# Hashed attention and a maxout FFN on one core: who sets the ones of the weight tiles, and where hashes and FFN groups stand in the order of work

## The chip, the core and the metric

The kernel runs on one core of a Trainium2 chip. The metric is the device time of one execution in microseconds (us). Five engines work beside each other, each through its own queue in order: TensorE (PE in the profile, its weight loads PEld), VectorE (DVE), ScalarE (ACT), GpSimd (POOL) and SyncE (SP), which here only issues DMAs.

## What is computed

Attention in which a query sees only the keys of its own hash bucket (six sign bits of a projection), and a feed-forward layer with a maximum over three branches, on 3072 tokens (4 batches x 768, 8 heads of 64):

```python
q_bits = (np.einsum('bhsd,dk->bhsk', q, proj) > 0).astype(np.int64)   # 6 bits; k_bits in the same way
mask = q_bucket[:, :, :, None] == k_bucket[:, :, None, :]
scores = np.where(mask, scale * np.matmul(q, k.transpose(0, 1, 3, 2)), -1e9)
attn = np.exp(scores - np.max(scores, axis=-1, keepdims=True))
attn = attn / (np.sum(attn, axis=-1, keepdims=True) + 1e-09)
x = np.matmul(attn, v)                       # then (b, s, h*d) = 3072 x 512
h = np.maximum(np.maximum(x @ w1, x @ w2), x @ w3)    # 512 -> 768
out = h @ w_out                                       # 768 -> 512
```

## The kernel before, in words

**Bits instead of a mask.** Each head's keys and queries lie as columns of a tile `S`: 64 rows hold the scaled vector and some rows below it hold the hash bits as plus or minus one half. One matmul over all rows gives the score plus a term that is largest where all bits agree, and the exponential (L303, with a bias) drives all other pairs to nothing.

**Units.** A unit is a piece of scores: one head, one chunk of queries, some blocks of 128 keys. Batch 0 has three chunks of 256 queries and 16 units per chunk; the other batches have two chunks of 384 and 24 units per chunk. That makes 192 units, 48 a batch, and chunks 0 to 8. For each unit `scores` (L279) issues the matmuls (L295, three of 256 columns or two of 384) into one of two PSUM buffers, takes a weight tile from the list `at_free`, and ScalarE writes the exponentials into it (L303). There are 24 weight tiles `AT`, used in turn.

**Ones in the weight tiles.** Behind each block of 256 or 384 columns stand two columns of ones; where a chunk is the first of its batch and half, the values' matmuls read one of them too (`n = w + 1`, L368), which gives the sum of the values. The tiles start in the form of batch 0 (blocks of 256). When a tile is first taken for a block of 384, the ones lie elsewhere, and `scores` has VectorE set them (L300 to L302), just ahead of the exponential on ScalarE.

**Bursts.** When four heads of a chunk (a half, i = 0 or 1) are through, a burst follows (L338): sums of the weights by a matmul with ones (L350), VectorE's transposes and reciprocal (L357 to L361), and the weighted values in two sides (L372), normalised by VectorE into `xT` (L379). Sums and values use four 32-column tiles of TensorE beside each other. From chunk 3 on VectorE adds the weights of a head's units first (L326, and L329 from chunk 5 on), so that fewer sums are left to TensorE. At the end of the burst's second side the weight tiles are given back to `at_free` (L382 to L385). In batch 0 the bursts of the second half are placed at units 32, 40 and 48; from chunk 3 on one comes every 12 units: 63, 75, 87, 99, 111, 123, 135, 147, 159, 171, 183 and one after the last unit.

**FFN groups.** When a chunk is complete its FFN is cut into groups (L390): 18 of four matmuls (L401; a copy of the first branch, then two maxima on VectorE, L406 to L410) and, per 128 rows, two halves of three matmuls (L445), the second of which ends with a copy on ScalarE and a store. At each unit a credit of 1 (batch 0) or 1.15 groups is spent from the list `ffn`. What is left of it when the units are through, and the whole FFN of chunk 8, come behind the last burst (L604 to L609). Scores, hashes, bursts and FFN groups that need a PSUM bank beside the score buffers share four of them, taken and given back in turn.

**Hashes.** Heads of batch 0 are turned on TensorE and hashed in pairs or one by one (L166 to L184), with the copies split over engines. From group 2 on (a group is four heads; groups 2g and 2g+1 belong to batch g) GpSimd or SP loads the group (L187), VectorE transposes it in four steps a side (L200), GpSimd narrows it (L205), SP places it into `S` (L210), TensorE hashes it (L219), VectorE makes bits (L222), and SP sends them into `S` (L230), at least one unit later. Which unit each of these steps stands at is written by hand: for groups 4 to 7 the first transpose is at `SPREAD[batch][0]` and they are `SPREAD[batch][1]/4` units apart, loads start 14 units before, and the hash stands at `need - 9`, where `need` is the unit that first reads the group's scores (96, 108, 144, 156).

**The order.** The whole order is the order of the calls (`manual_schedule`). In the loop over units (L586) each turn issues the scores of the next unit, then the steps listed for this one (`at`), then FFN groups by credit, then bursts (`todo`), then a hash (`hash_at`). Ahead of the loop (L486 to L520) stands the start: the first head's two sides are turned, copied, placed and hashed in two halves each, and score 0 is issued.

Of the kernel before, what the change touches and what calls it, by code (L numbers as in the profile page):

```python
# [17 lines left out]
def kernel(  # L18
# [12 lines left out]
    nc = tc.nc  # L31
# [4 lines left out]
    HALF = S // 2  # L36
# [14 lines left out]
    SCALE = 0.125 / (RS * RS)  # L51
    EPS = 2.0 ** -60
    NAT = 24
    SPREAD = {2: (61, 9), 3: (100, 12)}
    THIRD_ADD = 5
    LAG = (1, 4)
    ATW = 776
# [23 lines left out]
    at_tiles = [konst.tile([P, ATW], FP16, name=f"AT{i}", tag=f"AT{i}") for i in range(NAT)]  # L81
# [8 lines left out]
    def bank():  # L90
        i = free_banks.pop(0)
        return i, bank_tiles[i]

    def give(i):
        free_banks.append(i)
# [23 lines left out]
    def pair_turn(pi, side, hd, mp):  # L119
        n = nat[pi].rearrange("p (s h w) -> p s h w", s=2, h=2)  # L120
        for i in range(MH):
            nc.tensor.transpose(mp[:, i * P : (i + 1) * P], n[:, side, hd, i * P : (i + 1) * P], iden[:])  # L122
# [132 lines left out]
    def parts_of(c):  # L255
        return chunks[c][2] * NM // (2 * HALF)
# [4 lines left out]
    NU = len(units)  # L261
# [5 lines left out]
    at_free = list(range(NAT))  # L267
    at_form = [THIRD] * NAT
    at_of = {}
    xts, sv_of = {}, {}  # L270

    def blocks(t, w):
        nb = 2 * HALF // w
        return t[:, 0 : nb * (w + 2)].rearrange("p (n c) -> p n c", n=nb)

    def block_of(b, m):
        return 2 * (m % MH) + m // MH if b == 0 else m

    def scores(u):  # L279
        c, h, part = units[u]  # L280
        b, q0, w = chunks[c]
        nb = 2 * HALF // w
        (qn, qx), (kn, kx) = where[0, b * H + h], where[1, b * H + h]
        bits = NBITS if b == 0 else KB
        sc = sc_ps.tile([P, 2, 512], FP32, tag="sc", name="sc")
        if w == HALF:
            views = [sc[:, j, 0:w] for j in range(nb)]
            whole = sc[:, :, 0:w]
        else:
            flat = sc.rearrange("p a c -> p (a c)")  # L290
            views = [flat[:, j * w : (j + 1) * w] for j in range(nb)]
            whole = flat[:, 0 : nb * w].rearrange("p (n c) -> p n c", n=nb)
        for j in range(nb):
            m = nb * part + j
            nc.tensor.matmul(views[j], s_of[kn][0 : D + bits, kx, m * P : (m + 1) * P],  # L295
                             s_of[qn][0 : D + bits, qx, q0 : q0 + w], start=True, stop=True)
        i = at_free.pop(0)
        at_of[u] = i
        t = blocks(at_tiles[i], w)
        if at_form[i] != w:  # L300
            nc.vector.memset(t[:, :, w : w + 2], 1.0)
            at_form[i] = w  # L302
        nc.scalar.activation(t[:, :, 0:w], whole, ActFn.Exp, bias=-SCALE * 0.25 * bits, scale=SCALE)  # L303

    unit_at = {e: u for u, e in enumerate(units)}

    def weights_of(c, h, m):
        w = chunks[c][2]
        nb = 2 * HALF // w
        return blocks(at_tiles[at_of[unit_at[c, h, m // nb]]], w)[:, m % nb, :]  # L310
# [20 lines left out]
    def sum_blocks(c, h):  # L331
        w = chunks[c][2]
        if (c, h) in sum_of:
            t = sum_of[c, h]
            return [t[:, j, 0:w] for j in range(1 if c >= THIRD_ADD else 2)]
        return [weights_of(c, h, m)[:, 0:w] for m in range(NM)]

    def burst(c, i):  # L338
        b, q0, w = chunks[c]
        held = {}  # L340
        rb = []

        def sums(m0, m1):
            if m0 == 0:
                held["s"] = bank()
            sm = held["s"][1]
            bs = [sum_blocks(c, 4 * i + x) for x in range(4)]
            for m in range(len(bs[0])):
                for x in range(4):
                    nc.tensor.matmul(sm[Q * x : Q * (x + 1), 0:w], ones[:, :], bs[x][m],  # L350
                                     start=(m == 0), stop=(m == len(bs[0]) - 1))
            if m1 == NM:
                ys = ys_pool.tile([P, HALF], FP32, tag="ys", name="ys")
                rr = small.tile([P, HALF // Q], FP32, tag="rr", name="rr")
                n = w // Q
                rb.append(rb_pool.tile([P, HALF], FP32, tag="rb", name="rb"))
                nc.vector.transpose(ys[:, 0:w], sm[:, 0:w])  # L357
                give(held["s"][0])
                nc.vector.tensor_scalar(out=rr[:, 0:n], in0=ys[:, 0:w:Q], scalar1=EPS * S, scalar2=None, op0=AluOp.add)
                nc.vector.reciprocal(rr[:, 0:n], rr[:, 0:n])  # L360
                nc.vector.transpose(rb[0][:, 0:w], rr[:, 0:n].unsqueeze(2).to_broadcast((P, n, Q)))  # L361

        def values(side, m0, m1):
            if m0 == 0:
                held[side] = bank()
            av = held[side][1]
            first = (b, i, side) not in sv_of
            n = w + 1 if first else w  # L368
            for m in range(m0, m1):
                cb = block_of(b, m)  # L370
                for x in range(4):
                    nc.tensor.matmul(av[Q * x : Q * (x + 1), 0:n], v_at[2 * b + i][:, x, cb * D + side : (cb + 1) * D : 2],  # L372
                                     weights_of(c, 4 * i + x, m)[:, 0:n], start=(m == 0), stop=(m == NM - 1))
            if m1 == NM:
                if first:
                    sv_of[b, i, side] = small.tile([P, 1], FP32, tag=f"sv{side}", name="sv")
                    nc.vector.tensor_scalar(out=sv_of[b, i, side][:], in0=av[:, w : w + 1], scalar1=EPS, scalar2=None,
                                            op0=AluOp.mult)
                nc.vector.scalar_tensor_tensor(out=xt_of(c)[:, 2 * i + side, 0:w], in0=av[:, 0:w],  # L379
                                               scalar=sv_of[b, i, side][:], in1=rb[0][:, 0:w], op0=AluOp.add, op1=AluOp.mult)  # L380
                give(held[side][0])
                if side == 1:  # L382
                    for h in range(4 * i, 4 * i + 4):
                        for n in range(parts_of(c)):
                            at_free.append(at_of[unit_at[c, h, n]])  # L385

        return sums, values

# [71 lines left out]
    with tc.manual_schedule():  # L460
# [27 lines left out]
        ib, bk = bank()  # L488
# [13 lines left out]
        head_hash(mk, 0, 1, 0, (1,))  # L502
        head_bits(mk, 0, 1, 0, 1)
        give(ik)
        scores(0)
        pair_turn(0, 1, 1, bk)
        head_hash(mq, 0, 0, 0, (1,))
        head_bits(mq, 0, 0, 0, 1)
        give(iq)
        pair_turn(0, 0, 1, bq)  # L510
        pair_keep(0, 1, 1, bk)
        give(ib)
# [34 lines left out]
        hash_at = {}  # L547
        for g in range(2, NQUAD):
            b2, i2 = divmod(g, 2)
            need = UPB * b2 + 12 * i2  # L550
            for n, side in enumerate((1, 0)):
                name = (side, g)
                if g > 3:
                    us = [SPREAD[b2][0] + SPREAD[b2][1] * (8 * i2 + 4 * n + n2) // 4 for n2 in range(4)]
                    for x in range(4):
                        when(us[0] - 14 + x, load_quad, side, g, (x,), nc.gpsimd)
                else:
                    us = [need - {2: 26, 3: 23}[g] + 4 * n + n2 for n2 in range(4)]
                for n2, u2 in enumerate(us):
                    when(u2, turn, name, n2 // 2, n2 % 2)  # L560
                    if n2 % 2:
                        when(u2 + 1, narrow, name, n2 // 2)
                when(us[3] + 3, place, name, range(4))
            hash_at[{2: 33, 3: 47}.get(g, need - 9)] = g
            when({2: 36, 3: 46}.get(g, need - 22), load_v, g)

        ffn, credit = [], 0
        todo = {}
        last_of = {}
        for c, i in sorted(done_at, key=lambda e: done_at[e]):  # L570
# [3 lines left out]
            for n, f in enumerate(pieces):  # L574
                u = {(0, 0): (20, 21, 22), (1, 0): (24, 25, 26), (2, 0): (28, 29, 30)}.get((c, i), (d, d, d))[n]
# [8 lines left out]
                when(min(u + 2, NU - 1), add, c, h, n)  # L584

        for u in range(NU):  # L586
            if u + 1 < NU:
                scores(u + 1)
            for f in at.pop(u, []):
                f()  # L590
            for c in ffn_at.get(u, []):
                ffn += ffn_groups(c)
            credit += 1 if u < UPB else 1.15
            if not ffn:
                credit = 0
            while ffn and credit >= 1:
                credit -= 1
                ffn.pop(0)()
            for f in todo.pop(u, []):
                f()  # L600
            if u in hash_at:
                when(u + 1, quad_hash(hash_at[u]))

        for u in sorted(todo):  # L604
            for f in todo[u]:
                f()
# [33 lines left out]
```

## Time and profile before

| | |
|---|---|
| time, three runs | 272.11, 272.56, 272.76 us (median 272.56) |
| profiled execution | 272.63 us |
| its span, first to last instruction | 270.9 us |
| busy | PE 96%, PEld 57%, DVE 77%, ACT 66%, POOL 25% |
| granted TensorE clock | 1.00 in all 40 slices |
| HBM read, written | 25.17 MB, 6.29 MB |
| hashes of groups 2 to 7 start on TensorE at | 43.0, 57.7, 106.4, 124.4, 171.9, 187.9 us |

All positions in time are us from the span's start. In the view of waits a line names the waiting engine and line, what ended the wait, and then the total, the number of times and the longest. In a timeline a line has start, duration, engine, line, operation, tiles and shapes, count, and in brackets the idle time before it and what ended that. The busy digits are tenths in 40 slices of 6.8 us each.

### The profile page before, as it was taken

How to read it: one execution, taken by the hardware profiler on the slowest of the kernel's cores; microseconds unless marked ns; L12 is line 12 of the kernel's file. 1: busy time of each engine (PE TensorE's matmuls, PEld its weight loads, DVE VectorE, ACT ScalarE, POOL GpSimd, SP SyncE). 2: the span in 40 equal slices, each digit the busy share in tenths (PEclk: the TensorE clock that was granted, in tenths of full speed). 3: DMA queues.
4: the chain of work that ended last, by engine and by line, in shares of the span. 5: the costliest groups of instructions: out<-in, count | busy, mean ns of one | idle time of the engine just before them, and what ended most of it. 6: DMA issues, size and time to landing. Idle time of an engine off the chain costs nothing.

```text
span 270.9 us, 6455 instructions
## 1 busy us (share of the span) xinstructions
PE 259.4 (96%) x2505; PEld 154.5 (57%) x2505; DVE 208.9 (77%) x517; ACT 177.6 (66%) x257; POOL 68.4 (25%) x108
## 2 busy tenths in 40 slices
PE   7899999999989999979999999999999999998995
PEld 3555567865756575545555555565555655554553
DVE  2777686967699899948999998799849795887351
ACT  3587776676939693963959768484895859580322
POOL 3489641272032435140141512011000000000000
PEclk9999999999999999999999999999999999999999
DMA  6969999959623863980036291801130003000303
GB/s 204 315 137 160 221 255 229 229 80 250 150 72 88 156 173 38 235 218 20 11 91 202 30 205 69 169 11 46 29 116 2 2 2 116 2 0 2 116 0 116
DMA packets 20717, 30.95 MB, mean 114 GB/s; under 512 B 2608, under 2 KB 15248, under 8 KB 20688
## 3 DMA queue, kind: packets, MB, share of 16 engines
q0 software_dynamic: 8128, 13.37, 26.3%
q1 hardware_dynamic: 12128, 16.66, 21.1%
q10 hardware_dynamic: 432, 0.52, 0.5%
q8 instruction: 19, 0.31, 0.5%
q14 instruction: 10, 0.08, 0.1%
HBM read 25.17 MB, written 6.29 MB: 116 GB/s over the span
## 4 chain that ended last, share of the span: by engine, by line
PE 86%; DVE 5%; ACT 3%; DMA 2%; POOL 2%; issue 1%; SPq 0%; DVEq 0%; ACTq 0%; POOLq 0%
PE ms L401 32%; PE sc L295 22%; PE ms L372 11%; PE ms L445 10%; PE ms L350 3%; PE ms L219 3%; ACT AT L303 3%; DMA S<-bits 2%; PE ms L483 1%; POOL S L136 1%; PE ms L149 1%; PE ms L122 1%; DVE ad L326 1%; PE ms L169 1%; DVE S L174 1%
## 5 line engine op out<-in xcount | busy, mean ns | idle before, releaser
L303 ACT ACTIVATE AT<-sc 128x768 f16<-128x768 f32 x192 | 152.7, 816 | 65.6 <-PE sc L295 57.9
L401 PE MATMUL ms<-xT,w_sb 128*128 128x384 f16 (+1 forms) x648 | 115.0, 307 | 0.0
L295 PE MATMUL sc<-S 72*128 72x384 bf16 (+1 forms) x432 | 93.5, 308 | 5.4 <-ACT AT L303 2.5
L401 PEld LDWEIGHTS <-w_sb 128*128 128x128 f16 x648 | 62.6, 97 | 35.8 <-issue 0.3
L410 DVE TENSOR_TENSOR ht<-ht,ms 128x384 f16<-128x384 f16 (+1 forms) x108 | 54.2, 504 | 26.0 <-PE ms L401 23.1
L295 PEld LDWEIGHTS <-S 72*128 72x128 bf16 (+1 forms) x432 | 39.4, 98 | 38.0 <-issue 14.1
L205 POOL TENSOR_SCALAR T<-T 128x768 bf16<-128x768 f32 x24 | 22.9, 953 | 105.2 <-DVE T L200 64.5
L372 PE MATMUL ms<-AT,vo 128*32 128x385 f16 (+3 forms) x864 | 35.5, 309 | 0.0
L445 PE MATMUL ms<-wout_sb,ht 128*128 128x512 f16 x138 | 35.3, 378 | 0.0
L372 PEld LDWEIGHTS <-vo 128*32 128x32 f16 x864 | 22.8, 96 | 10.5 <-issue 2.9
L326 DVE TENSOR_TENSOR ad<-ad,AT 128x768 f16<-128x768 f16 x48 | 26.6, 553 | 1.8 <-ACT AT L303 1.1
L200 DVE STREAM_TRANSPOSE T<-nat 128x384 f32<-128x384 f32 x48 | 26.9, 565 | 0.0
L326 DVE TENSOR_TENSOR ad<-AT,AT 128x768 f16<-128x768 f16 x48 | 26.2, 546 | 0.4 <-ACT AT L303 0.4
L406 ACT CAST ht<-ms 128x384 f16<-128x384 f32 x36 | 17.2, 477 | 8.8 <-PE ms L401 8.8
L379 DVE SCALAR_TENSOR_TENSOR xT<-ms,sv,rb 128x384 f16<-128x384 f32 (+1 forms) x36 | 19.8, 567 | 1.6 <-PE ms L372 0.2
L445 PEld LDWEIGHTS <-ht 128*128 128x128 f16 x138 | 13.3, 97 | 13.0 <-DVE ht L410 0.4
L449 ACT COPY osb<-ms 128x512 f32<-128x512 f32 x21 | 12.2, 582 | 8.3 <-PE ms L445 7.2
L329 DVE TENSOR_TENSOR ad<-ad 128x384 f16<-128x384 f16 x32 | 15.5, 484 | 1.1
L136 POOL TENSOR_SCALAR S<-T 64x384 bf16<-64x384 f32 (+1 forms) x23 | 14.2, 617 | 4.7 <-DVE T L131 3.1
L357 DVE STREAM_TRANSPOSE ys<-ms 128x384 f32<-128x384 f32 (+1 forms) x18 | 9.6, 535 | 6.5 <-PE ms L350 6.4
L174 DVE TENSOR_SCALAR S<-ms 6x384 bf16<-6x384 f32 x16 | 8.9, 554 | 3.8 <-PE ms L169 3.5
L194 POOL DMA_DIRECT2D nat<-in_q_dram x20 | 11.1, 564 | 2.1 <-DMA vo<-in_v_dram 2.0
(48 smaller groups left out, 122.8 us busy)
## 6 DMA issues: line engine op xcount, KB each, us to landing
out_dram<-osb SPq DMA_DIRECT2D x21, 256.0 KB
S<-T SPq DMA_DIRECT2D x48, 96.0 KB
nat<-in_q_dram POOLq DMA_DIRECT2D x20, 192.0 KB, 7.3
vo<-in_v_dram POOLq DMA_DIRECT2D x8, 384.0 KB, 6.4
nat<-in_k_dram POOLq DMA_DIRECT2D x16, 192.0 KB, 6.5
w_sb<-in_moe_w_dram POOLq DMA_DIRECT2D x3, 768.0 KB, 7.6
nat<-in_k_dram SPq DMA_DIRECT2D x10, 192.0 KB
nat<-in_k_dram SPq DMA_DIRECT2D x3, 384.0 KB
```

The costliest lines, as they stand in the source:

```text
L136: nc.gpsimd.tensor_scalar(out=o, in0=i_, scalar1=RS, scalar2=1.0, op0=AluOp.mult, op1=AluOp.mult)
L200: nc.vector.transpose(t32[name][:, u, half * HALF : (half + 1) * HALF], i_)
L205: nc.gpsimd.tensor_scalar(out=t16[name][:, u, :], in0=t32[name][:, u, :], scalar1=RS, scalar2=1.0, op0=AluOp.mult, op1=AluOp.mult)
L295: nc.tensor.matmul(views[j], s_of[kn][0 : D + bits, kx, m * P : (m + 1) * P], s_of[qn][0 : D + bits, qx, q0 : q0 + w], start=True, stop=True)
L303: nc.scalar.activation(t[:, :, 0:w], whole, ActFn.Exp, bias=-SCALE * 0.25 * bits, scale=SCALE)
L326: nc.vector.tensor_tensor(out=sum_of[c, h][:], in0=t[0], in1=t[n], op=AluOp.add)
L372: nc.tensor.matmul(av[Q * x : Q * (x + 1), 0:n], v_at[2 * b + i][:, x, cb * D + side : (cb + 1) * D : 2], weights_of(c, 4 * i + x, m)[:, 0 ...
L379: nc.vector.scalar_tensor_tensor(out=xt_of(c)[:, 2 * i + side, 0:w], in0=av[:, 0:w], scalar=sv_of[b, i, side][:], in1=rb[0][:, 0:w], op0=A ...
L401: nc.tensor.matmul(ps[:, 0:w], w_sb[wi][:, jc, fb * P : (fb + 1) * P], xt[:, jc, 0:w], start=(jc == 0), stop=(jc == NJC - 1))
L406: nc.scalar.copy(hts[fb][:, 0:w], ps[:, 0:w])
L410: nc.vector.tensor_tensor(out=hts[fb][:, 0:w], in0=hts[fb][:, 0:w], in1=ps[:, 0:w], op=AluOp.max)
L445: nc.tensor.matmul(ps[:, 0:DM], hts[fb][:, tb * P : (tb + 1) * P], wout_sb[:, fb, :], start=(fb == 0), stop=(fb == NFB - 1))
```

## The change

The diff has four parts. The ones are set by GpSimd when the second-half bursts of batch 0 give their tiles back, and the tile is marked as being in the form of 384 columns. The hashes of groups 4 to 7 stand at `need - 12`, which are units 84, 96, 132 and 144 instead of 87, 99, 135 and 147, and the transposes of batch 3, with their loads, narrowings and placements, start at unit 97 instead of 100. The first three FFN groups that are left after the last unit are issued ahead of the last burst. In the start, the hash of the first head's second query half stands ahead of score 0, and score 1 directly behind score 0, instead of in the first turn of the loop.

```diff
-    SPREAD = {2: (61, 9), 3: (100, 12)}
+    SPREAD = {2: (61, 9), 3: (97, 12)}
...
                         for n in range(parts_of(c)):
-                            at_free.append(at_of[unit_at[c, h, n]])
+                            a = at_of[unit_at[c, h, n]]
+                            if b == 0 and i == 1:
+                                nc.gpsimd.memset(blocks(at_tiles[a], HALF)[:, :, HALF : HALF + 2], 1.0)
+                                at_form[a] = HALF
+                            at_free.append(a)
...
         head_bits(mk, 0, 1, 0, 1)
         give(ik)
-        scores(0)
-        pair_turn(0, 1, 1, bk)
         head_hash(mq, 0, 0, 0, (1,))
         head_bits(mq, 0, 0, 0, 1)
         give(iq)
+        scores(0)
+        scores(1)
+        pair_turn(0, 1, 1, bk)
         pair_turn(0, 0, 1, bq)
...
-            hash_at[{2: 33, 3: 47}.get(g, need - 9)] = g
+            hash_at[{2: 33, 3: 47}.get(g, need - 12)] = g
...
         for u in range(NU):
-            if u + 1 < NU:
+            if 0 < u < NU - 1:
                 scores(u + 1)
...
+        for f in ffn[:3]:
+            f()
+        ffn = ffn[3:]
         for u in sorted(todo):
             for f in todo[u]:
                 f()
```

## The prediction

> **What bounds the kernel now.** I read the busy times first, then the waits of TensorE, then the neighbourhood of each wait, because a busy share alone hides what a stage waits for.
>
> ```profile
> PE 259.4 (96%) x2505; PEld 154.5 (57%) x2505; DVE 208.9 (77%) x517; ACT 177.6 (66%) x257; POOL 68.4 (25%) x108
> ...
> PE   7899999999989999979999999999999999998995
> ...
> DVE  2777686967699899948999998799849795887351
> ```
>
> TensorE is busy nearly everywhere, so a microsecond is won only where it stands still or switches. The second candidate is VectorE, with nines from slice 10 to 17 (68 to 122 us). TensorE's own waits:
>
> ```profile
> PE sc L295 <- ACT AT L303: 2.5, 4, 1.2
> PE sc L295 <- DMA S<-bits: 1.7, 1, 1.7
> PE ms L350 <- DVE ad L329: 1.2, 1, 1.2
> ...
> PE ms L350 <- DVE ad L326: 0.4, 1, 0.4
> ```
>
> Drawn ends of matmuls are modelled, so I measure a loss by starts: in dense stretches the next matmul starts 0.109 us after one of 256 columns and 0.162 us after one of 384. What exceeds that is lost.
>
> **Part 1, ones by GpSimd (L301 goes; 24 memsets in the bursts of units 32, 40, 48).** ScalarE waits for VectorE's memset in the view of waits, and TensorE then waits for ScalarE to free a score buffer:
>
> ```profile
> ACT AT L303 <- DVE AT L301: 5.4, 4, 3.3
> ```
>
> (us in total, times, longest). The longest is this one, in the timeline:
>
> ```profile
> 80.64 1.62 ACT L303 ACTIVATE AT<-sc 128x768 f16<-128x768 f32 x2 [3.27 <-DVE AT L301]
> ```
>
> The memset ahead of it (80.45) takes 0.06 us, but it stands in VectorE's queue behind a burst's normalisation (77.43 to 80.42 here). By starts TensorE loses 80.00 to 81.50 less 0.11 = 1.39, in the same way 63.52 to 64.22 less 0.11 = 0.59, and 0.13 and 0.09 at 85 and 86: 2.20 us. On GpSimd each memset is 16 units ahead of its reader: tiles freed in the burst at 41 to 43 us are read by unit 48 (57.6), those at 60 to 62 by unit 64 (76.6). All 24 VectorE memsets disappear, since exactly these 24 tiles are the ones changing form. With the exponential of unit 65 starting at about 79.1 instead of 80.64, the next thing late is VectorE: the window 91 to 103 shows
>
> ```profile
> 91.00:103.00 12.00, 12.00 (x133) 8.56 (x132) 11.65 (x31) 9.13 (x12) 2.87 (x4) 1.00 0.69 154
> ```
>
> (busy PE, PEld, DVE, ACT, POOL: VectorE 11.65 of 12). It gains 0.59 itself before 68 us, about 0.03 for each memset taken from its saturated stretch (start to start of an add and the evacuation behind it: 0.47 with a memset between, 0.44 without), 0.4 in all, and an idle 0.95 at 89.6 to 90.6 where it waited for TensorE: 1.9 against TensorE's 2.2. I take **-2.2**, keep +0.2 for this friction, and as bounds -2.2 and -0.8 (VectorE takes the 1.39 back).
>
> GpSimd's price: its memsets take 0.10 to 0.20 us (rows L624, L518, 128x64 at 0.15). The added ones are bounded by these below and, above, by 0.55 us, a DMA issue on that engine. Behind them queue two loads of values, the narrowing of group 3 and the third and fourth quarter-loads of group 4's keys. The latter are the nearest due: issued at 59.1 and 59.65 now, they would follow the burst that ends at 62.1, so 62.1 + 8 x 0.15 + 2 x 0.56 = 64.4, landing 6.5 later (median of that group) at 70.9. The transpose that reads them starts at 73.84, or 73.25 after the gain: 2.3 us of cover, gone if one memset costs over 0.15 + 2.3/8 = 0.44.
>
> **Part 2, later hashes three units earlier.** Hash of group 4 (unit 87) comes behind a burst; its bits are issued by SP from 109.0 to 111.9 and TensorE stands until 117.15:
>
> ```profile
> 117.15 0.50 PE L295 MATMUL sc<-S 72*128 72x384 bf16 x2 [1.69 <-DMA S<-bits]
> ```
>
> By starts 115.13 to 117.15 less 0.16: **-1.85**. In unit 84 TensorE reaches the hash at 101.2 instead of 106.4; VectorE, 2 us behind there, gives bits at 103.6, SP's four issues (0.73 each) end by 106.6, ahead of the S placements now at 104.8, and with the 5.2 from last issue to landing now seen they are there by 112. Cover: 3 us. At 103.4 the burst waits 0.53 for an add; a hash of 1.5 us ahead of it gives VectorE that time, less 0.56 for the bits: **-0.5**, between -0.53 and +0.3. Groups 5, 6, 7 show no wait for bits now, so nothing is won there. Their new neighbour is the last transpose, two units before the hash (group 5: unit 94 and 96). Group 5's starts at 114.18 and ends at 114.75; TensorE would come to the hash at about 117.2: 2.4 us of cover. For group 7 the two-unit distance existed before (145, 147), and SPREAD's 97 keeps it (142, 144); its loads, narrowing and placements move by the same three units.
>
> But a hash is a job in 32-column tiles, like the burst. These rows price the switch (burst with hash, burst without, hash alone):
>
> ```profile
> 122.48 2.12 PE L372 MATMUL ms<-AT,vo 128*32 128x384 f16 x48
> 124.43 1.46 PE L219 MATMUL ms<-T,pj 128*32 128x384 f32 x16
> 125.83 0.50 PE L295 MATMUL sc<-S 72*128 72x384 bf16 x2
> ...
> 139.14 2.15 PE L372 MATMUL ms<-AT,vo 128*32 128x385 f16 x48
> 141.22 0.50 PE L295 MATMUL sc<-S 72*128 72x384 bf16 x2
> ...
> 42.56 0.50 PE L295 MATMUL sc<-S 70*128 70x256 bf16 x3
> 43.00 1.50 PE L219 MATMUL ms<-T,pj 128*32 128x384 f32 x16
> 44.43 0.50 PE L295 MATMUL sc<-S 70*128 70x256 bf16 x3
> ```
>
> Behind a burst: (125.83 - 122.48) - (141.22 - 139.14) = 3.35 - 2.08 = 1.27. Alone: 44.43 - (42.56 + 3 x 0.109) = 1.54. So each parted hash costs 0.27 more, four **+1.0** (bounds 0.8 and 1.1).
> The Trainium skill, "TensorEngine Tiling (Array Packing)", Key Properties, says that changing the tiling mode drains TensorE, which speaks against this part; it gives no price, and the rows agree in direction. By a reading without any drain the total would be 1.0 us lower.
>
> **Part 3, three FFN groups before the last burst.** TensorE starts a sum at 243.69 and the next at 245.19:
>
> ```profile
> 245.19 0.32 PE L350 MATMUL ms<-ad,ones 128*32 128x384 f16 x1 [1.16 <-DVE ad L329]
> ```
>
> The three groups are one of L401 (0.65) and two halves of L445 (0.65 each), 1.95 us, more than the gap of 1.5. They don't fill it whole: the sixth matmul of L445 reads the hidden tile whose last two maxima stand in VectorE's queue behind the adds, which end at 245.14; 0.5 each brings 246.1. TensorE would stand from 245.16 to about 246.15. Counting work, before: 245.19 + burst 2.2 + L401 0.65 + six halves 3.9 = 251.94; after: 246.35 + 2.3 + four halves 2.6 = 251.3. **-0.65**, between 0 and -1.35. The normalised tile now comes 1.07 us after the burst; the four halves (2.6) cover that.
>
> **Part 4, first hashes ahead of scores.** Score 0 waits anyway (7.94, behind placements and bits), so the moved hash is free. Score 1 goes from 9.81 to about 8.5 (its bits end at 8.39), the fourth bits from 9.61 to 8.4, the copies of the second heads from 10.19 to 9.25. Behind them TensorE is in order: two transposes, two groups, then score 2 at about 10.3 instead of 10.80; from exponential 2 (11.33) ScalarE runs without a long gap to 19.4. **-0.5**, between 0 and -1.1 (what the exponential of unit 1 wins).
>
> **Sum.** -2.2 + 0.2 - 1.85 - 0.5 + 1.0 - 0.65 - 0.5 = -4.5 us; from the profiled execution's 272.63 (span 270.9 and 1.7 around it), 268.1. The median of the runs is 272.56, 0.07 lower, so I say **268.0**.
>
> **Rivals.**
> VectorE takes it back: nines from 68 to 122 us speak for it, the idle 0.95 and the shifted hash against. It gives back 1.39 and 0.5: 269.9. Chance 0.17.
> Port: two VectorE adds (88.17 and 112.33) took 0.99 instead of 0.55 beside a narrowing on GpSimd. If each of the eight last memsets waits half a microsecond for VectorE, they take 8 x 0.7 = 5.6, the keys land at 75.3, 2 us late: 270.0. Chance 0.08.
> The Trainium skill, "SBUF — State Buffer", section "SBUF: two separate sides", says that GpSimd and VectorE share a port pair as an exclusive lock, and that a two-input VectorE operation conflicts only with a GpSimd one that reads; a memset reads nothing, so by it only the other VectorE modes could hold a memset up.
> More is won (tail fully covered, start 1.1): 266.7. Chance 0.10.
> Nothing moves, because the exponentials wait for GpSimd as they did for VectorE: then only the other parts count against +1.0; with the tail and start at zero 271.9 to 272.6. Chance 0.04.
> **Slower:** the same queue on GpSimd, with memsets so slow that group 4's transposes hold VectorE, and everything behind them. Place: after unit 48's burst. Price: 8 x (m - 0.44) us. It ends above the time before from m = 1.0, where 4.5 is lost; at 1.3 it is 274.9. Rows of 0.10 to 0.20 speak against it. Chance 0.08.
> The forecast has 0.53.
>
> The range is **266.2 to 270.8**: the larger gain, both 270 rivals, and the bounds of start, tail and friction. A measurement here tells 0.2% (0.5 us). Faster 0.88, within 0.2% 0.04, slower 0.08.
>
> **What would show it.** No L301 on VectorE; ScalarE without a wait for ones at 80 us; no wait for bits at 115; hashes standing between scores; the last sums without their wait, but one in L445 before them; exponential 1 at 9.2. I am wrong if TensorE's waits for VectorE between 75 and 115 us grow by over 1 us, or the transposes of group 4 wait for their load.

## The result, and the profile after

The changed kernel takes 269.21 us (median of 4 runs, 268.47 to 270.15), beside 272.66 us for the kernel before on the same chips. The ratio is 0.9869, with a 95% interval from 0.9824 to 0.9915. The profiled execution took 269.23 us, with a span of 267.2. The forecast of 268.0 had the direction and the range (266.2 to 270.8) right; it promised 4.5 us, and 3.4 came.

In the changed file lines 386 and later have moved: L387 is GpSimd's memset, L405 is the old L401, L414 the old L410, L449 the old L445. From the page of the changed kernel, the busy times:

```profile
PE 259.1 (97%) x2505; PEld 153.5 (57%) x2505; DVE 208.7 (78%) x493; ACT 177.9 (67%) x257; POOL 70.1 (26%) x132
```

VectorE has 24 instructions less and GpSimd 24 more, and nobody's busy time has changed by 2 us. TensorE's own waits, from the view of waits (us in total, times, longest):

```profile
PE ms L449 <- DVE ht L414: 1.6, 3, 0.8
...
PE sc L295 <- ACT AT L303: 0.8, 2, 0.6
PE sc L295 <- DVE S L174: 0.8, 2, 0.6
```

The waits for bits and for the adds are gone, that for exponentials has shrunk from 2.5 to 0.8, and there is a new one: the output matmuls (L449) wait for hidden tiles on VectorE.

**Where the time went** can be read without any cause in mind from when the first score matmul of a unit starts (TensorE's L295) in each profile. Every change of the difference is a gain or a loss between two units:

| unit | before | after | difference | what lies between it and the row above |
|---|---|---|---|---|
| 0 | 7.94 | 7.86 | -0.08 | |
| 3 | 11.21 | 10.51 | -0.70 | part 4 |
| 32 | 39.57 | 38.88 | -0.69 | |
| 34 | 42.56 | 42.09 | -0.47 | a loss of 0.22 inside the burst of unit 32 |
| 52 | 64.22 | 63.15 | -1.07 | part 1: the wait at 63.5 |
| 62 | 73.34 | 72.11 | -1.23 | part 1, small waits |
| 68 | 82.31 | 79.65 | -2.66 | part 1: the wait at 80 |
| 74 | 88.00 | 86.16 | -1.84 | new waits for VectorE |
| 84 | 99.47 | 97.63 | -1.84 | |
| 90 | 109.00 | 106.68 | -2.32 | part 2: group 4's hash parted from the burst, adds no longer late |
| 94 | 112.69 | 110.71 | -1.98 | a new wait for VectorE |
| 96 | 117.15 | 113.32 | -3.83 | part 2: the wait for bits |
| 102 | 126.81 | 123.21 | -3.60 | group 5's hash parted from its burst |
| 138 | 174.25 | 170.89 | -3.36 | the same, group 6 |
| 150 | 190.92 | 187.81 | -3.11 | the same, group 7 |
| 191 | 241.97 | 238.85 | -3.12 | |
| last matmul | 267.43 | 263.84 | -3.59 | part 3 |

The lines that answer to those of the prediction, from the changed kernel's timeline. ScalarE at the place where it waited 3.27 us for ones:

```profile
77.94 3.88 ACT L303 ACTIVATE AT<-sc 128x768 f16<-128x768 f32 x5 [2.47 <-PE sc L295]
```

It now waits for the scores alone and runs five exponentials one behind the other. TensorE around group 4's hash and the burst of unit 87:

```profile
99.25 1.50 PE L219 MATMUL ms<-T,pj 128*32 128x384 f32 x16
100.68 0.50 PE L295 MATMUL sc<-S 72*128 72x384 bf16 x2
...
103.08 0.51 PE L350 MATMUL ms<-ad,ones 128*32 128x384 f16 x8
103.42 2.12 PE L372 MATMUL ms<-AT,vo 128*32 128x384 f16 x48
105.47 0.34 PE L295 MATMUL sc<-S 72*128 72x384 bf16 x1
```

The hash stands between scores, the eight sums run in one piece, and the bits are there when unit 96 needs them (its scores start at 113.32 without a wait). Before, the sums of unit 87's burst stood still behind the third:

```profile
103.40 0.34 PE L350 MATMUL ms<-ad,ones 128*32 128x384 f16 x3
104.09 0.48 PE L350 MATMUL ms<-ad,ones 128*32 128x384 f16 x5 [0.35 <-DVE ad L326]
```

From the first sum to the first value it took 1.03 us before and takes 0.34 now, so this wait cost 0.69. The prediction has 0.53, which is less by the 0.16 that two matmuls of 384 columns are apart elsewhere; but four sums in tiles beside each other start within 0.01 us of one another. The end:

```profile
241.13 1.24 PE L449 MATMUL ms<-wout_sb,ht 128*128 128x512 f16 x5
243.20 0.39 PE L449 MATMUL ms<-wout_sb,ht 128*128 128x512 f16 x1 [0.82 <-DVE ht L414]
243.52 0.35 PE L350 MATMUL ms<-ad,ones 128*32 128x384 f16 x4
```

The sums no longer wait; the sixth output matmul ahead of them does. The start:

```profile
7.86 0.49 PE L295 MATMUL sc<-S 70*128 70x256 bf16 x3 [0.60 <-DVE S L174]
8.55 0.49 PE L295 MATMUL sc<-S 70*128 70x256 bf16 x3 [0.20 <-DVE S L174]
```

And the new loss, TensorE first and then VectorE:

```profile
84.76 0.59 PE L449 MATMUL ms<-wout_sb,ht 128*128 128x512 f16 x2
85.94 0.39 PE L449 MATMUL ms<-wout_sb,ht 128*128 128x512 f16 x1 [0.58 <-DVE ht L414]
```

```profile
84.54 0.57 DVE L200 STREAM_TRANSPOSE T<-nat 128x384 f32<-128x384 f32 x1
85.03 0.52 DVE L326 TENSOR_TENSOR ad<-ad,AT 128x768 f16<-128x768 f16 x1
85.47 0.41 DVE L414 TENSOR_TENSOR ht<-ht,ms 128x256 f16<-128x256 f16 x1
```

The maximum that completes the hidden tile stands in VectorE's queue behind a transpose and an add; the matmul starts 0.06 us after it ends at 85.88. By starts TensorE loses 0.75 here and 0.32 at 109.0, in the next chunk's first output group. It loses 0.30 more ahead of a group of L405, which starts at 83.02, just behind another late maximum (82.56 to 82.97).

### The profile page after: what moved, and what is told of

It is laid out like the page before. It is cut to its first block, busy times and chain, and to the rows that moved or that the text cites. A ratio compares the mean times of both kernels' runs of the same rounds, so it can differ in the third digit from the quotient of the medians.

```text
span 267.2 us, 6472 instructions
## 1 busy us (share of the span) xinstructions
PE 259.1 (97%) x2505; PEld 153.5 (57%) x2505; DVE 208.7 (78%) x493; ACT 177.9 (67%) x257; POOL 70.1 (26%) x132
## 4 chain that ended last, share of the span: by engine, by line
PE 85%; DVE 8%; ACT 3%; issue 2%; DVEq 0%; ACTq 0%
PE ms L405 31%; PE sc L295 22%; PE ms L372 11%; PE ms L449 10%; PE ms L219 3%; PE ms L350 3%; ACT AT L303 3%; DVE ht L414 2%; DVE ad L326 2%; PE ms L487 1%; PE ms L149 1%; PE ms L122 1%; DVE T L131 1%; PE ms L169 1%; DVE xT L379 1%
## 5 line engine op out<-in xcount | busy, mean ns | idle before, releaser
L405 PE MATMUL ms<-xT,w_sb 128*128 128x384 f16 (+1 forms) x648 | 114.8, 307 | 0.1
L295 PE MATMUL sc<-S 72*128 72x384 bf16 (+1 forms) x432 | 93.5, 309 | 1.7 <-ACT AT L303 0.8
L405 PEld LDWEIGHTS <-w_sb 128*128 128x128 f16 x648 | 62.7, 97 | 35.9 <-issue 0.4
L414 DVE TENSOR_TENSOR ht<-ht,ms 128x384 f16<-128x384 f16 (+1 forms) x108 | 54.2, 503 | 21.6 <-PE ms L405 18.5
L295 PEld LDWEIGHTS <-S 72*128 72x128 bf16 (+1 forms) x432 | 39.2, 98 | 34.0 <-issue 14.8
L205 POOL TENSOR_SCALAR T<-T 128x768 bf16<-128x768 f32 x24 | 22.9, 952 | 91.9 <-issue 47.7
L449 PE MATMUL ms<-wout_sb,ht 128*128 128x512 f16 x138 | 36.0, 379 | 1.6 <-DVE ht L414 1.6
L326 DVE TENSOR_TENSOR ad<-ad,AT 128x768 f16<-128x768 f16 x48 | 26.5, 552 | 1.8 <-ACT AT L303 1.1
L326 DVE TENSOR_TENSOR ad<-AT,AT 128x768 f16<-128x768 f16 x48 | 26.2, 546 | 0.4 <-ACT AT L303 0.4
L410 ACT CAST ht<-ms 128x384 f16<-128x384 f32 x36 | 17.1, 476 | 8.8 <-PE ms L405 8.8
L449 PEld LDWEIGHTS <-ht 128*128 128x128 f16 x138 | 13.3, 97 | 15.6 <-DVE ht L414 3.0
L329 DVE TENSOR_TENSOR ad<-ad 128x384 f16<-128x384 f16 x32 | 15.5, 484 | 1.1
```

Of the source, the lines that this page charges most:

```text
L205: nc.gpsimd.tensor_scalar(out=t16[name][:, u, :], in0=t32[name][:, u, :], scalar1=RS, scalar2=1.0, op0=AluOp.mult, op1=AluOp.mult)
L326: nc.vector.tensor_tensor(out=sum_of[c, h][:], in0=t[0], in1=t[n], op=AluOp.add)
L329: nc.vector.tensor_tensor(out=t[:, 0, :], in0=t[:, 0, :], in1=t[:, 1, :], op=AluOp.add)
L405: nc.tensor.matmul(ps[:, 0:w], w_sb[wi][:, jc, fb * P : (fb + 1) * P], xt[:, jc, 0:w], start=(jc == 0), stop=(jc == NJC - 1))
L410: nc.scalar.copy(hts[fb][:, 0:w], ps[:, 0:w])
L414: nc.vector.tensor_tensor(out=hts[fb][:, 0:w], in0=hts[fb][:, 0:w], in1=ps[:, 0:w], op=AluOp.max)
```

## The experiments

**How they are compared.** The theory: all four parts do what they say, and what is missing was taken back by VectorE, which had used TensorE's stalls to catch up. The main rival: the new waits belong to the moved hashes or to the order of VectorE's queue. Differences of a few tenths are too small for the times (the runs of one kernel lie 0.25 to 2.2 us apart), but not for the starts on TensorE. Score 0 starts between 7.61 and 8.70 in these profiles, so "later" and "earlier" are counted from score 0's own start: the last matmul comes 259.49 us after it before the change and 255.98 after it. The loss of 0.2 to 0.3 in the burst of unit 32 is there in some profiles and not in others (last section); where it blurs a number I count from unit 34 on.

**Part 1 undone.** VectorE sets the ones again.

```diff
-                            a = at_of[unit_at[c, h, n]]
-                            if b == 0 and i == 1:
-                                nc.gpsimd.memset(blocks(at_tiles[a], HALF)[:, :, HALF : HALF + 2], 1.0)
-                                at_form[a] = HALF
-                            at_free.append(a)
+                            at_free.append(at_of[unit_at[c, h, n]])
```

> The changed kernel with part 1 alone undone (VectorE sets the ones again, in the scores). Theory: the ones themselves were worth 2.2 us and VectorE, saturated from 74 us on, took 1.1 back (waits of L445's sixth matmul for a hidden tile at 85 and 109 us). Then the first score matmuls of units 52 to 68 come 2.2 us later than in the changed kernel, those waits disappear, and the last matmul starts 1.0 to 1.2 us later than its 263.84: 264.9, time about 270.3. Rival: the waits at 85 and 109 come from the hash of group 4 that now stands ahead of them, not from the won time; then they stay, and the last matmul starts 2.2 us later, 266.0, time about 271.4.

Measured: 270.40 us, ratio to before 0.9917 (0.9891 to 0.9943). The waits are back:

```profile
PE sc L295 <- ACT AT L303: 2.5, 4, 1.2
```

From unit 34 to unit 68 TensorE falls 2.19 us behind the changed kernel, of which 0.80 come back by unit 74, because the waits at 82 to 85 are not there; at the end 1.40 are left. So 0.8 us of what part 1 wins at the stalls is given back to VectorE. But the wait at 109 stays (0.33 by starts, here at 110.3): that one isn't part 1's, and the theory was wrong on it.

**Part 1 alone, on the kernel before.** The edit is the reverse of the one above.

> The kernel before with part 1 alone (ones by GpSimd, nothing else). Theory: 2.2 us are won from unit 52 to 68, 0.8 go back to VectorE by unit 74; then the burst of unit 87 waits longer for its adds than the 0.53 it waited before, because no hash stands ahead of it: another 0.3 to 0.8 goes back; the wait for bits stays about 1.85, since the hash and the score that needs its bits come earlier alike. Last matmul 0.6 to 1.1 us earlier than before's 267.43, time about 271.9. Rival: VectorE gives back only what it did in the changed kernel: 1.4 us earlier, about 271.3.

Measured: 271.09 us, 0.9936 (0.9919 to 0.9952); last matmul 2.16 us earlier than before, more than the theory and its rival gave. The 0.8 goes back by unit 74 here too. The wait for adds at unit 87 is 0.69 by starts, unchanged, so the further loss that I expected isn't there. And the wait for bits fell from 1.85 to 1.19: from the hash's start to the score that has the bits it took 10.12 us here (104.88 to 115.00) and 10.78 before (106.37 to 117.15), with the same 0.67 to 0.73 for each of SP's issues, so their landing came sooner. How long the four small transfers take to land is not fixed; why was not traced further.

**Part 2 undone.** All hashes at `need - 9`, `SPREAD` 100.

> The changed kernel with part 2 alone undone (all hashes at need - 9, transposes of batch 3 from unit 100). Theory: the wait for bits comes back (1.85), the wait of unit 87's burst for its adds too (0.5 to 1), the extra changes into 32-column tiles go (1.0 us less), and the wait at 109 us (0.32) goes, which belongs to the moved hash; net 1.2 to 1.7 us later, time about 270.7. Rival: the wait at 109 belongs to VectorE's load in general and stays; then 1.7 to 2.0 later.

Measured: 269.82 us, 0.9882 (0.9866 to 0.9899). From unit 84 on the last matmul comes 1.08 us later than in the changed kernel, a little less than the theory's 1.2 to 1.7: the wait for bits (1.66) and the wait for adds (0.69) return, the four extra changes of tiles (0.94 in all) go, and the wait at 109 (0.33) is gone. That wait therefore belongs to the moved hash: with a hash no longer behind unit 87's burst, TensorE comes to the first output group sooner than VectorE has its last maximum. (This profile also lost 0.7 us more than the changed kernel's between 34 and 42 us, which no edit here touches: 0.39 in a wait for the bits of an earlier group and 0.32 in unit 32's burst.)

**Only group 4's hash moved.**

```diff
-    SPREAD = {2: (61, 9), 3: (97, 12)}
+    SPREAD = {2: (61, 9), 3: (100, 12)}
...
-            hash_at[{2: 33, 3: 47}.get(g, need - 12)] = g
+            hash_at[{2: 33, 3: 47, 4: 84}.get(g, need - 9)] = g
```

> The changed kernel with the hashes of groups 5 to 7 back behind their bursts (units 99, 135, 147, and the transposes of batch 3 from unit 100); only group 4's stays at unit 84. Theory: only group 4's bits were ever late, and each of the other three moved hashes costs 0.24 us for an extra change in and out of 32-column tiles; the last matmul starts 0.7 us earlier, 263.1, time about 268.5. Rival: the three hashes also relieve VectorE or ScalarE where they stand, and moving them back costs waits; then 263.8 or later.

Measured: 268.33 us, 0.9838 (0.9809 to 0.9868). The last matmul comes 0.76 earlier, 0.72 of it in three steps of 0.24 at the three hashes, and no new wait appears. Group 5's hash behind its burst again:

```profile
118.89 2.12 PE L372 MATMUL ms<-AT,vo 128*32 128x384 f16 x48
120.84 1.46 PE L219 MATMUL ms<-T,pj 128*32 128x384 f32 x16
122.24 0.50 PE L295 MATMUL sc<-S 72*128 72x384 bf16 x2
```

Burst and hash take 3.35 us from the first value to the next score, as before the change. In the changed kernel group 4's take 2.05 (103.42 to 105.47) and 1.52 (99.25 less 0.09 for the way in, to 100.68): 0.22 more by these rows. The extra change into 32-column tiles and out again is the whole cost.

**Copies on ScalarE.** The first branch's copies of chunks 1 and 2, which take load off VectorE.

```diff
-                    if w == HALF:
+                    if w == HALF or c > 0:
                         nc.scalar.copy(hts[fb][:, 0:w], ps[:, 0:w])
```

> The changed kernel with the first branch's copies of chunks 1 and 2 on ScalarE instead of VectorE (12 of 0.42 us). Theory: VectorE's backlog is what L445 waits for at 85 and 109 us; with 2.5 us less in each chunk's FFN the three lost stretches there (0.3, 0.75, 0.32) go, and the last matmul starts 1.0 to 1.4 us earlier than 263.84: 262.6, time about 268.0. Rival: it is the order of VectorE's queue alone (a transpose and an add just ahead of the last maximum), not its load: at most 0.4 us is won. Second rival: ScalarE, 9.2 of 10 us busy from 64 to 74, becomes late, and scores wait for it: not faster.

Measured: 268.30 us, 0.9840 (0.9804 to 0.9876). The three lost stretches are gone; of L449's waits only the one at the end is left:

```profile
PE ms L449 <- DVE ht L414: 0.8, 1, 0.8
```

From unit 34 on this wins 1.33 (0.30 and 0.76 by unit 74, 0.33 by unit 94, within some hundredths) and loses 0.34 between units 52 and 62, where scores wait for ScalarE (0.22 at 69 us, 0.13 at 72). So the waits are a matter of VectorE's load, and the second rival is right too, for a quarter of the gain: ScalarE is busy for 9.50 of the 10 us from 64 to 74.

**Two groups ahead of the last burst** instead of three (`ffn[:2]`).

> The changed kernel with two FFN groups ahead of the last burst instead of three. Theory: the third group (the second half of L445) waits 0.99 us for the last maximum on VectorE, behind the adds; without it TensorE fills 1.3 us, the burst starts when the adds end, and the wait shrinks to 0.1 to 0.3: the last matmul starts 0.6 to 0.9 us earlier, about 263.1, time about 268.5. Rival: the wait just moves to the sums (adds end at 242.0) or behind the burst: no change within 0.2.

Measured: 269.23 us, 0.9874 (0.9826 to 0.9922), which cannot be told from the changed kernel's 0.9869; on TensorE the last matmul comes 0.50 earlier than in the changed kernel, counted from unit 191. The wait has shrunk from 0.99 to about 0.5, not to 0.1 to 0.3. Around it:

```profile
242.23 0.53 PE L350 MATMUL ms<-ad,ones 128*32 128x384 f16 x4
242.30 1.21 DVE L414 TENSOR_TENSOR ht<-ht,ms 128x384 f16<-128x384 f16 x2
...
242.90 0.51 PE L372 MATMUL ms<-AT,vo 128*32 128x384 f16 x8
```

The sums lose 0.19, the step to the values another 0.3, and the first values start 0.05 us after the first of the two maxima ends (242.85). They take the PSUM bank that the order of the calls gives them next, which this maximum frees. That reading fits the times; it was not tried by itself.

**Part 3 undone** (no group ahead).

> The changed kernel with part 3 alone undone (no FFN group ahead of the last burst). Theory: part 3 was worth 0.5 us at the end, since the wait of the last sum (1.5) comes back and the wait of L445 (0.99) goes; nothing before the last unit changes. Last matmul 0.5 us later counted from score 0, time about 269.7. Rival: the time does not follow TensorE's last matmul there, because the last stores hang on ScalarE and the DMA: same time as the changed kernel within 0.2.

Measured: 269.88 us, 0.9879 (0.9834 to 0.9924). Counted from unit 34 the last matmul comes 0.47 later than in the changed kernel, with the sums' wait of 1.48 by starts back: part 3 is worth half a microsecond. The times differ by about as much (0.67), though they alone would not prove it.

**Part 4 undone** (the start as before).

> The changed kernel with part 4 alone undone (the start as before). Theory: the start was worth 0.62 to 0.69 us, and nothing behind it gives that back, since all later stages are chained to TensorE: from unit 3 on every score comes 0.6 to 0.7 us later than in the changed kernel, counted from score 0's own start, and so does the last matmul; time about 269.9. Rival: the loads, which fill the DMA queues from 20 to 40 us, set the pace behind the start; then the difference is gone by unit 48, and the time is the changed kernel's.

Measured: 270.14 us, 0.9900 (0.9878 to 0.9923). Scores come 0.61 later from unit 3 to unit 32 and 0.41 later from unit 34 to the end, and the 0.2 between is the loss in unit 32's burst, which this profile hasn't. Nothing behind the start gives the gain back.

**The three edits together**: group 4's hash alone, two groups ahead, and the copies on ScalarE only where it has room.

```diff
-                    if w == HALF:
+                    if w == HALF or c == 2 or (c == 1 and fb >= 3):
```

> The changed kernel with three edits together: only group 4's hash moved (the others behind their bursts), the first branch's copies on ScalarE for chunk 2 and for the last three hidden blocks of chunk 1, and two FFN groups ahead of the last burst. Theory: the savings add up, 0.72 for three hashes, 1.3 for the waits of L445 at 82 to 85 and 109 us without ScalarE's 0.35 at 69 to 72, 0.5 at the end: the last matmul 2.4 us earlier than in the changed kernel counted from score 0, time 266.7. Rival: with VectorE's waits gone ScalarE or the next wait takes part of it: 267.3 or more.

Measured: **267.12 us**, 0.9790 (0.9775 to 0.9805), below the changed kernel's interval. The last matmul comes 2.75 earlier, 2.47 from unit 34 on. In the window from 74 to 91 us, where the changed kernel's TensorE lost a microsecond (changed kernel, then this one),

```profile
74.00:91.00 17.00, 16.27 (x181) 10.22 (x182) 15.91 (x40) 11.91 (x16) 7.71 (x11) 1.00 0.40 94
74.00:91.00 17.00, 17.00 (x198) 10.69 (x196) 15.52 (x39) 12.62 (x20) 7.72 (x11) 1.00 0.46 103
```

(behind the length, TensorE's and, third, VectorE's busy time) TensorE is busy for all 17 us. On TensorE the savings add up; the time lies between the theory's 266.7 and the rival's 267.3.

**Group 4's hash behind a burst as well**, at unit 75, with batch 2's transposes earlier (`SPREAD` (58, 8), the combined kernel otherwise).

> The combined kernel (group 4's hash alone moved, copies on ScalarE, two groups ahead of the last burst) with batch 2's transposes from unit 58 on, two units apart, and group 4's hash at unit 75, behind that unit's burst. Theory: the last extra change into 32-column tiles goes (0.24), and the transposes fill VectorE's idle time before unit 60, so that nothing else moves: last matmul 0.25 us earlier than in the combined kernel counted from score 0, time 266.9. Rival: VectorE is late at the burst of unit 75, whose copies and adds then stand behind more transposes; TensorE waits there, and the time is 267.3 or more.

Measured: 268.51 us, 0.9823 (0.9770 to 0.9877). The theory fell. The wait is back, larger than ever:

```profile
84.91 0.60 PE L449 MATMUL ms<-wout_sb,ht 128*128 128x512 f16 x2
86.60 0.39 PE L449 MATMUL ms<-wout_sb,ht 128*128 128x512 f16 x1 [1.10 <-DVE ht L414]
```

By starts 1.27 and 0.39 are lost here. It is not at the burst that TensorE waits, as the rival had it, but where a hidden tile's last maximum is late, once more. The transposes are denser (one every two units), and with them GpSimd's narrowings moved, one of which now meets an add:

```profile
83.72 0.83 POOL L205 TENSOR_SCALAR T<-T 128x768 bf16<-128x768 f32 x1 [2.08 <-issue]
83.81 1.15 DVE L326 TENSOR_TENSOR ad<-AT,AT 128x768 f16<-128x768 f16 x1
```

The add takes 1.15 us instead of 0.55, and from it VectorE works without a pause up to the late maximum (86.14 to 86.54). So by an estimate from these lines 0.6 of the 1.27 is due to this meeting and the rest to the denser queue; no run separates the two. A place at VectorE between 74 and 91 us can cost more than the 0.24 of a change of tiles.

## Why the prediction was right, and where its size was off

**Part 1** was mis-sized in its friction. The stalls themselves were worth 2.19 (forecast 2.2), on GpSimd each memset took 0.10 us (estimate 0.15), and group 4's remaining loads were issued in time (62.64 and 63.18). But I let VectorE take back 0.2, by adding up how much earlier its queue could run. The runs showed 0.8. The sum failed because it asked whether VectorE's total work fits, and not how late it is at the one instruction that TensorE needs next. The first rival's mechanism is thus true in part (it gave 1.9 back; 0.8 came). My own sign of being wrong, waits for VectorE between 75 and 115 us that grow by over 1 us, was nearly met: by starts the new ones are 1.37, and 0.69 for the adds went. The transposes of group 4 did not wait for their load.

**Part 2**: the wait for bits was worth 1.85 in this pair of profiles, as forecast; that it fits to the hundredth is luck, since the same wait took 1.19 and 1.66 in two other profiles with the old hashes. Group 4's other terms (adds no longer late, a hash parted) came to -0.48, where I had -0.5 and +0.27: the hash cost 0.22, and the adds' wait was worth 0.69 and not 0.53, as read above. Each of the other three cost 0.24 (forecast 0.27). What I missed is the wait of 0.33 at 109: I looked at what the moved hash delays and not at what follows the burst that it leaves. That work now starts about 1.4 us sooner after the burst.
The Trainium skill, "TensorEngine Tiling (Array Packing)", Key Properties, has the drain at a change of tiling mode; the trace agrees, with 0.24 us for the way in and out.

**Part 3** came to 0.48 (forecast 0.65) for the reason given: the sixth output matmul waited for the maximum behind the adds. The two maxima ended 1.13 us behind the adds (242.02 to 243.14), where I had 0.96, and that is the 0.17 that is missing. That the wait came out at 0.99, just as I had it, is luck: I also let TensorE arrive 0.17 too early (at 245.16, where its place counted from unit 191 is 245.33).

**Part 4** came to 0.61 (forecast 0.5): score 2 started at 10.18, where I had 10.3, and later stages kept it.

**The sum.** On TensorE 3.59 instead of 4.5: 0.61 and 0.33 too little for VectorE, 0.22 for the loss in unit 32's burst, 0.17 at the end, less 0.19 in the start (score 0 itself came 0.08 sooner) and 0.26 in group 4's adds and the hashes. The rest of 1.1 lies behind the last matmul, where the profiled execution took 5.39 us instead of 5.20.

**The rivals.** The port rival didn't come: all 24 memsets took 97 to 103 ns beside VectorE's normalisations and transposes. The Trainium skill, "SBUF — State Buffer", section "SBUF: two separate sides", would let a two-input VectorE operation hold up only a GpSimd one that reads. No run here shows that for a memset, since the first add begins at 63.69 and the last memset at 62.14. The slower rival needed 1.0 us a memset. The exponentials don't wait for GpSimd: the one such line in the waits (2.1 at 62.21) ends 0.60 us after its score matmuls start, where 0.53 to 0.59 is the usual distance.

## What to carry to other kernels

When a stall is removed, look up what the next-busiest engine did during it. If it was catching up, part of the gain can come back as a wait at the first instruction that needs its latest result, however well its total work fits (here 0.8 of 2.19 us). A job that shares a tile mode with its neighbour should be moved away only if its result is late: of four moved hashes one paid. And to fill a gap with work ahead of it, take only as much as does not hang on the engine that made the gap.

## What the runs showed of the hardware that was not expected

In the burst of unit 32, ahead of the last matmul of the values' first side (at about 41 us), TensorE stood 0.2 to 0.3 us longer than before in the changed kernel, in the one with only group 4's hash moved and in the one with two groups ahead; 0.14 with the hash at unit 75; 0.55 with part 2 undone; and not at all in the other seven profiles, five of which have the same memsets on GpSimd. So it is not the change that makes it. The view of waits names no releaser there. The traces have a candidate: the queue that the page lists as `instruction` (q8, 19 packets) moves 16 KB a packet. In the kernel before and the changed one a packet comes, from 72 us on, once in 218 to 292 of TensorE's matmuls and weight loads, and in every profile one comes just ahead of this burst. It ends 0.69 to 0.91 us after the start of unit 32's scores in the five profiles with the loss and 0.36 to 0.61 us after it in the seven others. That sorts all twelve, but no run tests it, and the cause stays open.

An add of VectorE that begins while GpSimd narrows (L205) is held until the narrowing has ended. In all twelve profiles every such add of 128x768 (L326) ends 0.40 to 0.44 us after the narrowing, whenever it began; the longest took 1.15 us instead of 0.55, and two in the kernel before and two in the changed one took 0.99 (the first at 88.17 and at 86.91). Those of 128x384 (L329), eight in each, end 0.20 to 0.21 us after it and take 0.86 to 0.87 instead of 0.36. An add that already runs when the narrowing begins takes 0.51 to 0.52, no more than others. Nothing of VectorE grew beside GpSimd's memsets; its adds begin only after them, so that pair was not seen.
